# Block 2 of a fused attention and GEGLU kernel: output products at its opening, other loading order for batches 3 and 4, earlier sums of the output weights

## The chip, the cores and the metric

The kernel runs on one core of a Trainium2 chip. A core has five engines that work side by side, each through its own list of instructions in the order of the program: TensorE (PE in the profile) multiplies matrices out of SBUF into PSUM, VectorE (DVE) and ScalarE (ACT) work elementwise and read PSUM, GpSimd (POOL) works elementwise on SBUF, and SyncE (SP) here only issues DMA transfers. An instruction waits for semaphores of the work it depends on, and all that stands behind it in its engine's list waits with it. The metric is the device time of one execution in microseconds (us); lower is better. Several executions are made, and their median is the time of a kernel.

## What is computed

Eight batches go through a linear attention with eight heads, and its result through a gated feed-forward layer. Cut to what matters:

```python
# q, k, v: (8, 8, 576, 64) float32; w_gate, w_val: (512, 1536); w_out: (1536, 512)
theta = np.pi / 2.0 * pos / S
def phi(x): r = np.maximum(x, 0.0); return np.concatenate([r * cos_w, r * sin_w], axis=-1)
q_p, k_p = phi(q), phi(k)
kv  = np.einsum('bhsf,bhsd->bhfd', k_p, v)
z   = np.sum(k_p, axis=2)
num = np.einsum('bhsf,bhfd->bhsd', q_p, kv)
den = np.einsum('bhsf,bhf->bhs', q_p, z)[..., None] + 1e-06
x   = (num / den).transpose(0, 2, 1, 3).reshape(B * S, H * D)     # 4608 x 512
g   = x @ w_gate
out = (0.5 * g * (1.0 + erf(g / sqrt(2))) * (x @ w_val)) @ w_out   # 4608 x 512
```

## The kernel before

**Tiles and stages.** The 4608 rows of x are taken as nine blocks of 512 (`BLK`, `n` = 0 to 8), the 1536 hidden columns as twelve units of 128 (`JT`, `jt` = 0 to 11; "unit 3" is `jt` 3). A batch has 576 rows, so blocks and batches do not coincide: block 2 holds rows 1024 to 1535, which are the end of batch 1 and the first 384 rows of batch 2; block 3 begins in batch 2 and goes on into batch 3. The batches are therefore prepared one or two blocks ahead, between the units of an earlier block.

**A batch's way to x.** `load` (L98) brings q, k and v as float32 into the three slots of `st`, or into the spare tiles `sm` and `fs`; `stage` says which. `prep` (L177 on ScalarE, L179 on VectorE) clips at zero and multiplies with the sine or cosine of the position, one of nine groups of rows `j` at a time, into `phis`; `prep_both` (L191, L193) does it for q and k together. `cast_v` (L208) copies v into `vx`. `turn_q` (L222) transposes q with two DMAs on SyncE. `kv_unit` (L270) makes the products of k and v with 72 matmuls and copies them out on ScalarE (L279). `nm_unit` (L311 on TensorE, L322 to L324 on VectorE) makes 128 rows of the numerators, divides them by the denominators and writes an x tile; eight small matmuls into two PSUM banks from `b0` on. These steps together are called "numerators" below. `turn_x` (L378) transposes the x tile into `xT` of its block by DMA, on SyncE.

**A unit.** `gv_unit` (L430) multiplies a block's xT with 128 columns of the gate weights and of the value weights, four matmuls each of 512 columns, into two PSUM banks in turn (0 and 1, then 2 and 3). ScalarE takes the GELU of the gate part (L439, tile `gel`, two buffers), VectorE multiplies it with the value part into `hT` (L442). The next but one unit writes the same two banks. Units 0 and 1 of block 1 and units 0 to 3 of block 2 are made in two halves of 256 columns; block 2 makes the first halves of units 0 to 3, then the second halves.

**Output products.** The output of block `n - 1` is made during block `n`. For blocks 1 to 8 it uses a scheme of seven products in place of eight (`PROD`): `product` (L547) multiplies parts of hT, or sums of them (`h_sum`, L529, `SUMS` says at which step, tile in `sm`), with parts of the output weights, or differences of them (`wo_sum`, L492, four on VectorE, made once in block 1; "T1" overwrites a part of `wo_sb`). ScalarE copies some products (L565), VectorE adds them (L560). `o_step` makes one step of products: step 0 and step 6 have two products (12 matmuls), the others one (6 matmuls). In block 2 step 0 is products 2 and 1; product 2 reads hT of units 6 to 11 of block 1.

**What sets the order.** The order is written out by hand; there is no scheduler. `block1` and `block2` walk through the units; after each unit they call the small pieces that stand at that number. `LOADS` says after which (block, unit) loads of a batch are put on SyncE (with a range of `j`, or of heads), `SCALE` which groups of q and k of which batch are scaled (numbers from 12 on are units 0 on of block 2; the first tuple is sines on ScalarE, the second cosines on VectorE), `EARLY` which groups of batch 4 (`s` sines on ScalarE, `c` cosines, from unit 9 on also on ScalarE). `more` puts the sums of xT for block 3 (L630) on GpSimd after units 8 to 11 of block 2; from block 3 on the units too use a seven-product scheme (L650). All DMAs named here but a few of the first stage go through SyncE in order, so a turn of q, whose two issues take some 8 to 9 us of SyncE, holds up every load and x transpose behind it.

Around block 2 SyncE's order before is: turn of q of batch 2; the last x tile of batch 1; k of batch 3 and the first half of v; x tile 0 of batch 2; the second half of v; x tiles 1 and 2; q and k of batch 4, groups 0 to 4; turn of q of batch 3; x tiles 3 and 4; the rest of q and k and v of batch 4.

Of the kernel before, what the change touches and what calls it, by code (L numbers as in the profile page):

```python
# [16 lines left out]
def kernel(  # L17
# [13 lines left out]
    nc = tc.nc  # L31
# [6 lines left out]
    JT = J // 128  # L38
# [45 lines left out]
    def stage(name, b):  # L84
        early = {
            ("q", 1): 1, ("k", 1): sm, ("v", 1): fs, ("k", 2): 2, ("v", 2): 1,
            ("q", 3): fs, ("k", 3): 2, ("v", 3): sm,
            ("q", 5): 1, ("k", 5): 0, ("q", 7): 1, ("k", 7): 0,
        }
        at = early.get((name, b), "qkv".index(name))  # L90
        if isinstance(at, int):
            return st[:, at]
        return at[:, 0:NP * R * D].rearrange("p (m x) -> p m x", m=NP)
# [113 lines left out]
    def cast_v(b, m0, m1, copy, j0=0, j1=R):  # L207
        copy(  # L208
            vx[:, m0:m1, j0:j1, 0:D],
            staged["v", b][:, m0:m1, j0 * D:j1 * D].rearrange("p m (j d) -> p m j d", d=D),  # L210
        )
# [97 lines left out]
    def nm_unit(b, t, b0=6):  # L309
        for h in range(H):  # L310
            nc.tensor.matmul(  # L311
                bank(b0 + h // 4)[:, (h % 4) * (D + 1):(h % 4 + 1) * (D + 1)],
                lhsT=q_cols(b, t, h),
                rhs=kv_sb[b][:, h // 2, h % 2, :],
                start=True,
                stop=True,
            )
        nm = ps[:, b0:b0 + 2, 0:4 * (D + 1)].rearrange("p g (h d) -> p g h d", h=4)
        den = attn2.tile([128, 2, 4], FP32, name="den")
        rec = attn2.tile([128, 2, 4], FP32, name="rec")  # L320
        x = xsp.tile([128, 2, 4, D], BF16, name="x_sb")
        nc.vector.tensor_scalar_add(den, nm[:, :, :, D], EPS)  # L322
        nc.vector.reciprocal(rec, den)
        nc.vector.tensor_tensor(  # L324
            x,
            nm[:, :, :, 0:D],
            rec[:, :, :, None].to_broadcast([128, 2, 4, D]),
            op=ALU.mult,
        )
        xs[b, t] = x.rearrange("p g h d -> p (g h d)")  # L330
# [153 lines left out]
    def wo_sum(name):  # L484
        if not ts:
            ts["B11"], ts["B12"] = wo_sb[:, 0:JH, 0:CH], wo_sb[:, 0:JH, CH:C]
            ts["B21"], ts["B22"] = wo_sb[:, JH:JT, 0:CH], wo_sb[:, JH:JT, CH:C]
        x, y = {
            "T1": ("B12", "B11"), "T2": ("B22", "T1"), "T3": ("B22", "B12"), "T4": ("T2", "B21"),
        }[name]  # L490
        ts[name] = ts["B12"] if name == "T1" else weights.tile([128, JH, CH], BF16, name=name)
        nc.vector.tensor_tensor(ts[name], ts[x], ts[y], op=ALU.subtract)  # L492
# [403 lines left out]
    def js(a, b):  # L896
        return tuple(range(a, b))

    LOADS = {
        (1, 4): [(3, "k"), (3, "v", 0)], (1, 9): [(3, "v", 2)],  # L900
        (1, 11): [(4, "q", 0, 5), (4, "k", 0, 5)],
        (2, 2): [(4, "q", 5, R), (4, "k", 5, R), (4, "v")],
        (2, 9): [(5, "q", 0, 5), (5, "k", 0, 5)],
        (3, 1): [(5, "q", 5, R), (5, "k", 5, R), (5, "v")],
        (3, 9): [(6, "q", 0, 5), (6, "k", 0, 5)],
        (4, 0): [(6, "q", 5, R), (6, "k", 5, R), (6, "v")],
# [1 line left out]
        (5, 0): [(7, "q", 5, R), (7, "k", 5, R), (7, "v")],  # L908
    }
    SUMS = {  # L910
        2: {0: "1", 1: "2", 2: "34", 3: "56", 6: "78"},
        8: {i: str(i + 1) for i in range(8)},
    }
    for n in range(3, 8):
# [44 lines left out]
    def scale(b, name, sines_, cosines):  # L959
# [8 lines left out]
        5: (3, "q", js(0, 1), ()), 6: (3, "q", js(1, 3), js(0, 1)),  # L968
        7: (3, "q", js(3, 5), js(1, 3)), 8: (3, "q", js(5, 7), js(3, 6)),
        9: (3, "q", js(7, 9), js(6, 9)),  # L970
        10: (3, "k", js(0, 2), js(0, 2)), 11: (3, "k", js(2, 4), js(2, 4)),
        12: (3, "k", js(4, 6), js(4, 6)), 13: (3, "k", js(6, 8), js(6, 8)),
        14: (3, "k", js(8, 9), js(8, 9)),
    }

    def block1():
        b, n = 2, 1
        for jt in range(JT):
            i = jt - 9
            if i > 0:  # L980
                nm_unit(b, i, (6, 4, 6)[i])
                turn_x(b, i)
            if jt < 2:
                for i in range(2):
                    half, unit = divmod(2 * jt + i, 2)
                    x3 = lambda: turn_x_pe(1, 3, 5, dve_copy)
                    gv_unit(n, unit, half * HALF, HALF, between=x3 if jt == i == 0 else None)
                    j = JA + 2 * jt + i
                    prep("q", b, 1, (j,), eng=nc.scalar)
                    prep("q", b, 0, (j,))  # L990
            else:
                gv_unit(n, jt, between=(lambda: nm_unit(b, 0, 6)) if i == 0 else None)
            if i == 0:
                turn_x(b, 0)
            if jt % 3 == 1:
                flush()
            if jt == 2:
                prep("q", b, 0, (R - 1,))
                prep("q", b, 1, (R - 1,), eng=nc.scalar)
                turn_q(b)  # L1000
                nm_unit(1, NT - 1)
            if jt == 3:
                turn_x(1, NT - 1)
            if jt == 6:
                kv_unit(b)
            if jt in SCALE:
                scale(*SCALE[jt])
            if jt in (3, 4):
                cast_v(b, 2 * (jt - 3), 2 * (jt - 3) + 2, act_copy)
            if jt == 11:  # L1010
                cast_v(3, 0, 2, act_copy)
            start_loads(n, jt)
            if 4 <= jt < 8:
                wo_sum(("T3", "T1", "T2", "T4")[jt - 4])

    EARLY = {
        4: "s0 c0", 5: "s1 c1", 6: "s2 c2", 7: "s3 c3", 8: "s4 c4", 9: "s5 c5", 10: "s6 c6",
        11: "s7 c7", 12: "s8 c8",
    }

    def early(jt):
# [3 lines left out]

    def block2():
        b, n = 3, 2
        for jt in range(JT):
            if jt >= 4:
                gv_unit(n, jt, to=(2, 6) if jt == JT - 1 else None)  # L1030
            else:
                for i in range(2):
                    half, unit = divmod(2 * jt + i, 4)
                    gv_unit(n, unit, half * HALF, HALF)
                    if i == 0 and jt < 2:
                        nm_unit(2, 3 + jt)
                    if i == 0 and jt == 1:
                        turn_q(3)
            if 0 <= jt - 6 < NT:
                turn_x(b, jt - 6)  # L1040
            if jt == 0:
                cast_v(b, 2, 4, act_copy)
            if jt < JT - 1:
                o_step(n, jt)
            if 0 <= jt - 5 < NT:
                nm_unit(b, jt - 5)
            if jt + JT in SCALE:
                scale(*SCALE[jt + JT])
            if jt == 3:
                kv_unit(b)  # L1050
            early(jt)
            if jt == 1:
                turn_x(2, 3)
                turn_x(2, 4)
            start_loads(n, jt)
            if jt in (7, 8):
                m = 2 * (jt - 7)
                cast_v(4, m, m + 2, act_copy)
            more(n, jt)

    turn[0] = 1
# [128 lines left out]
```

## Time and profile before

| | before |
|---|---|
| three runs | 311.64, 311.2, 310.38 us; median 311.2 |
| the profiled execution | 312.38 us |
| its span (first to last instruction on the engines) | 310.6 us |
| TensorE busy | 298.2 us, 96% of the span, 3071 matmuls |
| VectorE, ScalarE, GpSimd busy | 228.1, 202.2, 153.4 us |
| granted TensorE clock, mean | 0.985 |
| x transposes between 54 and 126 us, issue to landing | 2.5 / 3.6 / 7.0 us (least, median, most) |
| turns of q there, issue to landing | 6.6 / 6.9 / 8.1 us each of two |
| loads into `st` there, issue to landing | 3.9 / 5.2 / 7.6 us |
| cast of half a batch's v (L208), ScalarE and GpSimd | 1149 and 1150 ns |

A busy TensorE is not one at full speed: matmuls are pipelined, a matmul of 512 columns starts 0.216 us after the one before it although one lasts 0.36 us by itself, and the clock that the throttle grants can fall. Block 1 runs from 55.7 to 79, block 2 from 81.5 to 116.8 us of the profiled execution, block 3 begins at 116.8. A time of a run is some 1.8 us above the span of its profile, and the profiled execution lies above the three runs shown.

### The profile page before, as it was taken

To read this page: it belongs to the slowest core of one execution; us is meant where nothing else is said; L and a number is where in the kernel's file an instruction comes from. 1 tells how busy PE (TensorE), PEld (TensorE's weight loads), DVE (VectorE), ACT (ScalarE), POOL (GpSimd) and SP (SyncE) were. 2 spreads that over 40 slices of the span, in tenths; PEclk is the share of its full clock that TensorE was granted. 3 is DMA by queue.
4 is the path that set the end of the run, shared out by engine and by line. 5 is a ranking of instruction groups with operands and counts; after the bars stand their busy time and mean duration, and the time that the engine had idled before them with its cause. 6 is when DMAs were issued, how large, how long until landed. Compare 5 with 4: busy or idle time off the path is not lost.

```text
span 310.6 us, 7905 instructions
## 1 busy us (share of the span) xinstructions
PE 298.2 (96%) x3071; PEld 226.9 (73%) x3071; DVE 228.1 (73%) x495; ACT 202.2 (65%) x394; POOL 153.4 (49%) x130
## 2 busy tenths in 40 slices
PE   8799999999799999999999999999999999999993
PEld 3574456755486557787878787878888988888882
DVE  5675996889776864789678967895678785766772
ACT  7765593997654397878587858785546456565530
POOL 6585430000000049646864686579965866297310
PEclk9799999999899999999999999999999999999998
DMA  7999999998988889995989699936732321203045
GB/s 268 250 182 236 322 302 396 267 155 209 257 191 109 272 193 223 134 342 149 192 157 329 155 198 132 341 85 111 121 78 48 83 43 36 58 12 70 0 87 118
DMA packets 73172, 53.66 MB, mean 173 GB/s; under 512 B 45392, under 2 KB 62544, under 8 KB 73136
## 3 DMA queue, kind: packets, MB, share of 16 engines
q1 hardware_dynamic: 63360, 41.17, 58.5%
q0 software_dynamic: 9696, 11.93, 16.8%
q8 instruction: 24, 0.39, 0.5%
q14 instruction: 12, 0.10, 0.1%
q10 hardware_dynamic: 80, 0.07, 0.1%
HBM read 37.75 MB, written 9.44 MB: 152 GB/s over the span
## 4 chain that ended last, share of the span: by engine, by line
PE 78%; DMA 6%; issue 5%; DVE 4%; ACT 2%; SPq 2%; POOL 1%; POOLq 0%; DVEq 0%; ACTq 0%
PE ps L650 29%; PE ps L547 19%; PE ps L430 18%; DMA st<-in_v_dram 5%; PE ps L463 3%; PE ps L311 3%; PE ps L270 2%; DMA xT<-x_sb 2%; PE ps L233 1%; SPq L98 1%; DVE hT L442 1%; ACT phis L177 1%; PE ps L401 1%; ACT gel L439 1%; PE ps L386 1%
## 5 line engine op out<-in xcount | busy, mean ns | idle before, releaser
L630 POOL TENSOR_TENSOR fs<-xT 128x512 bf16<-128x512 bf16 x12 | 13.9, 1159 | 78.3 <-ACT gel L439 68.5
L430 PE MATMUL ps<-xT,wg_sb 128*128 128x512 bf16 (+1 forms) x208 | 48.6, 357 | 2.3 <-DMA xT<-x_sb 2.3
L430 PE MATMUL ps<-xT,wv_sb 128*128 128x512 bf16 (+1 forms) x208 | 48.7, 357 | 0.0
L529 POOL TENSOR_TENSOR sm<-hT 128x768 bf16<-128x768 bf16 x24 | 39.4, 1641 | 17.0 <-PE ps L650 9.9
L442 DVE TENSOR_TENSOR hT<-gel,ps 128x512 bf16<-128x512 f32 (+1 forms) x52 | 32.3, 623 | 16.0 <-PE ps L430 10.9
L650 PE MATMUL ps<-fs,ws 128*128 128x256 bf16 x288 | 41.7, 273 | 0.0
L650 PEld LDWEIGHTS <-ws 128*128 128x128 bf16 x384 | 36.2, 98 | 4.6 <-ACT ps L669 0.3
L439 ACT ACTIVATE gel<-ps 128x512 f32<-128x512 f32 (+1 forms) x52 | 28.5, 548 | 13.7 <-PE ps L430 12.3
L682 ACT ACTIVATE gel<-ps 128x512 f32<-128x512 f32 x30 | 17.9, 597 | 30.0 <-PE ps L650 30.0
L547 PEld LDWEIGHTS <-sm 128*128 128x128 bf16 x336 | 32.9, 98 | 5.9
L650 PE MATMUL ps<-xT,wg_sb 128*128 128x256 bf16 x240 | 36.0, 273 | 0.0
L690 DVE TENSOR_TENSOR ps<-fs,ps 128x512 f32<-128x512 f32 x30 | 20.9, 696 | 20.0 <-PE ps L650 13.7
L547 PEld LDWEIGHTS <-hT 128*128 128x128 bf16 x288 | 28.7, 100 | 5.7
L430 PEld LDWEIGHTS <-wv_sb 128*128 128x128 bf16 x208 | 20.4, 99 | 16.8
L560 DVE TENSOR_TENSOR o_sb<-sm,ps 128x256 f32<-128x256 f32 x56 | 23.4, 419 | 12.0 <-ACT sm L565 10.0
L430 PEld LDWEIGHTS <-wg_sb 128*128 128x128 bf16 x208 | 19.3, 98 | 15.8 <-issue 2.8
L529 POOL TENSOR_TENSOR sm<-hT,sm 128x768 bf16<-128x768 bf16 x12 | 19.7, 1644 | 15.5 <-PE ps L547 13.1
L324 DVE TENSOR_TENSOR x_sb<-ps,rec 128x512 bf16<-128x512 f32 x38 | 26.3, 691 | 1.3
L650 PEld LDWEIGHTS <-wg_sb 128*128 128x128 bf16 x240 | 23.1, 98 | 5.4
L177 ACT ACTIVATE phis<-st,sin_t 128x256 bf16<-128x256 f32 (+1 forms) x57 | 23.9, 480 | 3.3 <-DMA st<-in_k_dram 3.3
L191 ACT ACTIVATE phis<-st,sin_t 128x512 bf16<-128x512 f32 x36 | 25.8, 717 | 0.0
L547 PE MATMUL ps<-wo_sb,hT 128*128 128x256 bf16 x192 | 24.7, 279 | 0.0
(127 smaller groups left out, 590.9 us busy)
## 6 DMA issues: line engine op xcount, KB each, us to landing
out_dram<-o_sb SPq DMA_DIRECT2D x69, 128.0 KB, 3.1
st<-in_v_dram SPq DMA_DIRECT2D x10, 576.0 KB, 7.2
st<-in_q_dram SPq DMA_DIRECT2D x5, 640.0 KB, 4.5
st<-in_q_dram SPq DMA_DIRECT2D x5, 512.0 KB, 5.0
st<-in_k_dram SPq DMA_DIRECT2D x4, 640.0 KB, 6.0
st<-in_k_dram SPq DMA_DIRECT2D x4, 576.0 KB, 4.2
st<-in_q_dram POOLq DMA_DIRECT2D x4, 576.0 KB, 12.6
st<-in_k_dram SPq DMA_DIRECT2D x4, 512.0 KB, 4.9
```

Of the source, the lines that this page charges most:

```text
L177: nc.scalar.activation(o, i, AF.Relu, scale=tab[:, j:j + 1])
L191: nc.scalar.activation(o, i, AF.Relu, scale=tab[:, j:j + 1])
L324: nc.vector.tensor_tensor(x, nm[:, :, :, 0:D], rec[:, :, :, None].to_broadcast([128, 2, 4, D]), op=ALU.mult,)
L430: nc.tensor.matmul(bank(to[g])[:, 0:w], lhsT=wt[:, ct, js], rhs=xt[:, ct, c0:c0 + w], start=(ct == 0), stop=(ct == CT - 1),)
L439: nc.scalar.activation(gel[:, 0:w], bank(to[0])[:, 0:w], AF.Gelu)
L442: nc.vector.tensor_mul(hT[n][:, jt, c0:c0 + w], gel[:, 0:w], bank(to[1])[:, 0:w])
L529: eng.tensor_tensor(a[name][:, j0:j1], a[x][:, j0:j1], a[y][:, j0:j1], op=op)
L547: nc.tensor.matmul(at, lhsT=hs.setdefault(key, h_parts(n, p))[a][:, j], rhs=ts[b][:, j], start=(j == 0 and i in ((1, 2, 4, 5), (1, 4, 5))[ ...
L560: nc.vector.tensor_tensor(o, got[key, k], x, op=op)
L650: nc.tensor.matmul(to[:, 256 * half:256 * half + 256], lhsT=w_part(a, j * 128, (j + 1) * 128)[:, ct], rhs=xb[self.n][b][:, ct], start=(hal ...
L682: nc.scalar.activation(self.gel0, self.other, AF.Gelu)
L690: nc.vector.tensor_tensor(bank(val), self.m5, self.sum, op=ALU.add)
```

## The change

Everything lies in blocks 1 and 2.

- `block2` makes output step 0 ahead of its first unit, not after unit 0; the numerators of x tile 3 of batch 2 move from block 2's unit 0 to the end of block 1, those of tile 4 from unit 1 to unit 0, and the turn of q of batch 3 with them. The banks of numerators 0, 1, 2 in block 1 change from 6, 4, 6 to 4, 6, 4.
- The four sums of the output weights move from units 4 to 7 of block 1 to units 0 to 3.
- v of batch 3 goes to `fs` (where q of batch 3 lay) instead of `sm`. Its first half is loaded after unit 9, its second after unit 11, each behind the x tiles of that unit. The last x tile of batch 1 is turned after unit 5, behind k of batch 3.
- Cosines of k of batch 3 leave block 1's units 10 and 11; sines go three, two, two, one, one and cosines three, three, three from block 2's unit 0 on. The casts of v of batch 3 move to block 2's units 1 and 2.
- The first groups of q and k of batch 4 are loaded after block 2's unit 0, behind the turn of q of batch 3, instead of after block 1's unit 11. Their scaling starts at unit 6 instead of unit 4, with one more cosine on ScalarE. v of batch 4 is cast on GpSimd after units 8 and 9, instead of on ScalarE after units 7 and 8. The first groups of batch 5 are loaded after unit 10 instead of 9.
- One sum of hT moves from step 6 to step 4 of block 2.

```diff
--- before.py
+++ after.py
@@ -84,7 +84,7 @@
     def stage(name, b):
         early = {
             ("q", 1): 1, ("k", 1): sm, ("v", 1): fs, ("k", 2): 2, ("v", 2): 1,
-            ("q", 3): fs, ("k", 3): 2, ("v", 3): sm,
+            ("q", 3): fs, ("k", 3): 2, ("v", 3): fs,
             ("q", 5): 1, ("k", 5): 0, ("q", 7): 1, ("k", 7): 0,
         }
         at = early.get((name, b), "qkv".index(name))
@@ -897,10 +897,10 @@
         return tuple(range(a, b))
 
     LOADS = {
-        (1, 4): [(3, "k"), (3, "v", 0)], (1, 9): [(3, "v", 2)],
-        (1, 11): [(4, "q", 0, 5), (4, "k", 0, 5)],
+        (1, 4): [(3, "k")], (1, 9): [(3, "v", 0)], (1, 11): [(3, "v", 2)],
+        (2, 0): [(4, "q", 0, 5), (4, "k", 0, 5)],
         (2, 2): [(4, "q", 5, R), (4, "k", 5, R), (4, "v")],
-        (2, 9): [(5, "q", 0, 5), (5, "k", 0, 5)],
+        (2, 10): [(5, "q", 0, 5), (5, "k", 0, 5)],
         (3, 1): [(5, "q", 5, R), (5, "k", 5, R), (5, "v")],
         (3, 9): [(6, "q", 0, 5), (6, "k", 0, 5)],
         (4, 0): [(6, "q", 5, R), (6, "k", 5, R), (6, "v")],
@@ -908,7 +908,7 @@
         (5, 0): [(7, "q", 5, R), (7, "k", 5, R), (7, "v")],
     }
     SUMS = {
-        2: {0: "1", 1: "2", 2: "34", 3: "56", 6: "78"},
+        2: {0: "1", 1: "2", 2: "34", 3: "56", 4: "7", 6: "8"},
         8: {i: str(i + 1) for i in range(8)},
     }
     for n in range(3, 8):
@@ -968,9 +968,9 @@
         5: (3, "q", js(0, 1), ()), 6: (3, "q", js(1, 3), js(0, 1)),
         7: (3, "q", js(3, 5), js(1, 3)), 8: (3, "q", js(5, 7), js(3, 6)),
         9: (3, "q", js(7, 9), js(6, 9)),
-        10: (3, "k", js(0, 2), js(0, 2)), 11: (3, "k", js(2, 4), js(2, 4)),
-        12: (3, "k", js(4, 6), js(4, 6)), 13: (3, "k", js(6, 8), js(6, 8)),
-        14: (3, "k", js(8, 9), js(8, 9)),
+        10: (3, "k", js(0, 3), ()), 11: (3, "k", js(3, 5), ()),
+        12: (3, "k", js(5, 7), js(0, 3)), 13: (3, "k", js(7, 8), js(3, 6)),
+        14: (3, "k", js(8, 9), js(6, 9)),
     }
 
     def block1():
@@ -978,7 +978,7 @@
         for jt in range(JT):
             i = jt - 9
             if i > 0:
-                nm_unit(b, i, (6, 4, 6)[i])
+                nm_unit(b, i, (4, 6, 4)[i])
                 turn_x(b, i)
             if jt < 2:
                 for i in range(2):
@@ -989,7 +989,7 @@
                     prep("q", b, 1, (j,), eng=nc.scalar)
                     prep("q", b, 0, (j,))
             else:
-                gv_unit(n, jt, between=(lambda: nm_unit(b, 0, 6)) if i == 0 else None)
+                gv_unit(n, jt, between=(lambda: nm_unit(b, 0, 4)) if i == 0 else None)
             if i == 0:
                 turn_x(b, 0)
             if jt % 3 == 1:
@@ -999,23 +999,23 @@
                 prep("q", b, 1, (R - 1,), eng=nc.scalar)
                 turn_q(b)
                 nm_unit(1, NT - 1)
-            if jt == 3:
+            if jt == 5:
                 turn_x(1, NT - 1)
             if jt == 6:
                 kv_unit(b)
+            if jt < 4:
+                wo_sum(("T3", "T1", "T2", "T4")[jt])
             if jt in SCALE:
                 scale(*SCALE[jt])
             if jt in (3, 4):
                 cast_v(b, 2 * (jt - 3), 2 * (jt - 3) + 2, act_copy)
             if jt == 11:
-                cast_v(3, 0, 2, act_copy)
+                nm_unit(b, 3, 6)
             start_loads(n, jt)
-            if 4 <= jt < 8:
-                wo_sum(("T3", "T1", "T2", "T4")[jt - 4])
 
     EARLY = {
-        4: "s0 c0", 5: "s1 c1", 6: "s2 c2", 7: "s3 c3", 8: "s4 c4", 9: "s5 c5", 10: "s6 c6",
-        11: "s7 c7", 12: "s8 c8",
+        6: "s0 c0 s1 c1", 7: "s2 c2 s3", 8: "c3 s4", 9: "c4 s5", 10: "c5 s6", 11: "c6 s7",
+        12: "c7 s8 c8",
     }
 
     def early(jt):
@@ -1025,6 +1025,7 @@
 
     def block2():
         b, n = 3, 2
+        o_step(n, 0)
         for jt in range(JT):
             if jt >= 4:
                 gv_unit(n, jt, to=(2, 6) if jt == JT - 1 else None)
@@ -1032,20 +1033,19 @@
                 for i in range(2):
                     half, unit = divmod(2 * jt + i, 4)
                     gv_unit(n, unit, half * HALF, HALF)
-                    if i == 0 and jt < 2:
-                        nm_unit(2, 3 + jt)
-                    if i == 0 and jt == 1:
+                    if jt == i == 0:
+                        nm_unit(2, 4)
                         turn_q(3)
             if 0 <= jt - 6 < NT:
                 turn_x(b, jt - 6)
-            if jt == 0:
-                cast_v(b, 2, 4, act_copy)
-            if jt < JT - 1:
+            if 0 < jt < JT - 1:
                 o_step(n, jt)
             if 0 <= jt - 5 < NT:
                 nm_unit(b, jt - 5)
             if jt + JT in SCALE:
                 scale(*SCALE[jt + JT])
+            if jt in (1, 2):
+                cast_v(b, 2 * jt - 2, 2 * jt, act_copy)
             if jt == 3:
                 kv_unit(b)
             early(jt)
@@ -1053,9 +1053,9 @@
                 turn_x(2, 3)
                 turn_x(2, 4)
             start_loads(n, jt)
-            if jt in (7, 8):
-                m = 2 * (jt - 7)
-                cast_v(4, m, m + 2, act_copy)
+            if jt in (8, 9):
+                m = 2 * (jt - 8)
+                cast_v(4, m, m + 2, nc.gpsimd.tensor_copy)
             more(n, jt)
 
     turn[0] = 1
```

## The prediction

> **What bounds the kernel now.** I read the page first, then TensorE's waits, the chain of waits near the longest of them, and there the timeline and one-microsecond windows.
>
> ```profile
> span 310.6 us, 7905 instructions
> PE 298.2 (96%) x3071; PEld 226.9 (73%) x3071; DVE 228.1 (73%) x495; ACT 202.2 (65%) x394; POOL 153.4 (49%) x130
> ```
>
> TensorE is the bound; only its idle or slow time can be won. Its waits (engine, line, what for: total us, times, longest):
>
> ```profile
> PE ps L430 <- DMA xT<-x_sb: 2.3, 1, 2.3
> ...
> PE ps L311 <- DVE x_sb L324: 0.8, 2, 0.5
> ```
>
> All three lie where this change works: the first at block 2's opening, the other two in block 2. The chain of waits there (start, us, what) runs through VectorE into one transposing DMA:
>
> ```profile
> 74.46 0.79 DVE phis L179 x3
> 75.25 0.09 DVE den L322
> ...
> 76.31 5.07 DMA xT<-x_sb
> 81.39 0.14 issue
> 81.52 1.03 PE ps L430 x8
> ```
>
> The timeline shows what that wait cost and who stood beside it:
>
> ```profile
> 78.17 1.03 PE L430 MATMUL ps<-xT,wv_sb 128*128 128x512 bf16 x4
> ...
> 79.44 0.91 ACT L177 ACTIVATE phis<-st,sin_t 128x256 bf16<-128x256 f32 x2 [2.46 <-DMA st<-in_k_dram]
> ...
> 80.26 0.58 ACT L439 ACTIVATE gel<-ps 128x512 f32<-128x512 f32 x1
> ...
> 81.03 0.68 DVE L442 TENSOR_TENSOR hT<-gel,ps 128x512 bf16<-128x512 f32 x1
> ```
>
> ScalarE waited 2.46 us for k of batch 3, so unit 11's GELU came at 80.26 and its hT at 81.03. In the windows (length, PE, PEld, DVE, ACT, POOL, granted clock, DMA share, GB/s) the clock falls after the idle time:
>
> ```profile
> 80.00:81.00 1.00, 0.00 (x0) 0.00 (x0) 0.93 (x4) 1.00 (x3) 0.00 (x0) 1.00 0.59 123
> 81.00:82.00 1.00, 0.48 (x5) 0.46 (x6) 1.00 (x4) 1.00 (x3) 0.00 (x0) 1.00 1.02 348
> 82.00:83.00 1.00, 1.00 (x17) 0.86 (x15) 0.25 (x2) 0.95 (x2) 0.00 (x0) 0.86 1.14 303
> 83.00:84.00 1.00, 1.00 (x6) 0.75 (x5) 0.93 (x4) 0.34 (x2) 0.00 (x0) 0.50 0.85 126
> ```
>
> Later in the timeline stand the two L311 waits, with ScalarE's wait for v of batch 4 between them:
>
> ```profile
> 106.45 0.42 PE L311 MATMUL ps<-kv_sb,qT 128*128 128x65 bf16 x8 [0.25 <-DVE x_sb L324]
> ...
> 108.96 1.16 ACT L208 CAST vx<-st 128x1152 bf16<-128x1152 f32 x1 [3.04 <-DMA st<-in_v_dram]
> ...
> 112.42 0.42 PE L311 MATMUL ps<-kv_sb,qT 128*128 128x65 bf16 x8 [0.54 <-DVE x_sb L324]
> ```
>
> What there is to win, in the profiled execution:
> - Idle at the opening: matmuls of 512 columns start 0.216 us apart, so TensorE was free at 78.17 + 0.86 = 79.03 and went on at 81.52: 2.49.
> - Slow clock: from 82.65 to 86.50 (3.85 us) it did a half unit (0.87 at full clock, 86.50 to 87.37) and 12 output products (1.31, 102.08 to 103.39): 3.85 - 2.18 = 1.67.
> - The two L311 waits: products begun at 105.38 and 111.07 take 0.66, the numerators came at 106.45 and 112.42: 0.41 + 0.69 = 1.10. The second follows ScalarE's late cast, whose wait held unit 8's GELU until 110.02.
>
> Sum 5.26. After 117 us TensorE shows no further wait, so a shift there reaches the end.
>
> **The change, part by part.** Steps between VectorE's operations are read from its timeline, start to next start, as 0.87 for a weight sum:
>
> ```profile
> 69.19 0.95 DVE L492 TENSOR_TENSOR wo_sb<-wo_sb 128x1536 bf16<-128x1536 bf16 x1
> 70.06 0.68 DVE L442 TENSOR_TENSOR hT<-gel,ps 128x512 bf16<-128x512 f32 x1
> ```
>
> So also hT 0.59 (0.33 for a half unit), three cosines 0.79 (one 0.33), one set of numerators (L322 to L324) 1.04.
>
> *Weight sums into units 0 to 3.* VectorE was busy there already. Counted on from 57.38, with a sum after each of units 0 to 3: the last cosine of q of batch 2 ends 0.4 later (62.6), hT of unit 3 ends at 65.99, of unit 4 at 68.24. The value products of units 5 and 6 need those banks; they began at 65.67 and 67.39, and now at 66.05 and 68.30: 0.91, of which 0.10 was already spent waiting for v's cast ahead of kv (68.25 to 68.35). Cost 0.8. Bounds: 0 if VectorE's steps close up, 4 x 0.87 = 3.5 if no sum is hidden.
>
> *Block 2 opens with products.* Numerators 3 of batch 2 (0.26) and 12 products (1.31) now fill the wait for x. But the products need unit 11's hT. VectorE, freed of the sums, starts hT of unit 8 when TensorE ends it (73.25 + 0.05) and then does 4 x 0.59 + 2 x 0.79 + 3 x 1.04 = 7.06; with the last one's end (0.10) and handover (0.06), 80.52, against TensorE free at 79.03 + 0.26 = 79.29. New idle 1.23, both ends moved by the 0.8. Bounds: 0.71 (hT 11 alone: 79.20 + 0.05 + 0.69 + 0.06) and 1.9 (k late, rival 2). The first half unit then starts at 79.29 + 1.23 + 0.8 + 1.31 = 82.63 with 1.57 of work behind it that stood ahead at 81.52: 83.09 - 82.63 = 0.46 won.
>
> *k ahead of v, v behind the x tiles, cosines of k out of block 1.* SyncE's turn of q (62.48, 8.33 us) starts 0.4 later, so k is issued at 71.2 and 71.7 (72.81 before). Its halves landed 4.9 and 6.0 us after issue, with v behind them; so 77.7 at the latest, when the GELU of unit 10 ends on ScalarE. x 0 of batch 2 is ready at 76.6; with its 5.07 again it lands at 81.7, 0.9 before it is needed. v's first half waits on SyncE until q's last cosine leaves fs (78); behind it is x 1, ready only at 79. x 2, ready at 80.7, is needed at 82.63 + 4 x 0.87 + 0.26 + 0.66 = 87.0; its kind landed in 2.9 to 4.8 here. v's second half, issued near 82, lands by 89 (7.1 is the longest); ScalarE casts it near 90.5, kv follows at 91.8. The rest of batch 1's last x tile goes behind k, lands in 2.9 and is needed at 82.63. Numerators 2 read the banks that the products overwrite, but x 2 comes before hT 11 on VectorE. Taken as 0, because these covers stand; each us beyond them costs a us.
>
> *The clock.* The idle 1.23 stands in for 2.49. The nearest rows: the other fall (11 to 15 us) followed 1.25 + 0.17 + 0.51 us of idle, and 0.69 at 111.7 brought none. 1.23 is nearer to 0.69 than to 1.93: no fall, 1.67 won. Bounds 0 and 1.67.
>
> The Trainium skill ("TensorE: Matmul & The Clock Gate", section "Why this matters for your kernels") asks for no idle gap over about 3 us. By that rule neither gap would touch the clock, and the sum would be 1.67 smaller; the rows above disagree with it, since 2.49 brought 0.50.
>
> *Batch 4.* Its first loads go behind q's turn on SyncE, which now starts when numerators 4 of batch 2 end (83.9; 87.86 before) and takes 9.5: issued near 94 (82.43 before), landed by 100.6 (6.0). Two x transposes (1.25 each) later come the second halves (about 98; landing 5.1) and v (7.1): 104 and 107. First use is now VectorE after x 1 of batch 3, near 102.7, ScalarE's second halves after unit 9's GELU, near 108.8. Margins 2 and 4 us. The casts (2 x 1.15 on POOL, same length as ScalarE's) stand ahead of and between the x sums; T2 was ready 2.9 before its product, so 1.15 fits. One sum (0.47) leaves VectorE's unit 6. So the two L311 waits go, up to a rest of 0.1 (bounds 0 and 1.10). Batch 5's first loads, one unit later, are first used in block 3 near 120 and issued near 113 (landing 6.1): 0. ScalarE has one more cosine before the turn of q of batch 4, 0.6 later; that landed at 132.1 and is used at 132.93: 0.
>
> The skill's "SBUF — State Buffer" ("SBUF: two separate sides") has VectorE and GpSimd share a port pair that one instruction holds alone; by it a cast could hold a cosine for up to 1.15. No run here shows such a pair, and the sum leaves it out.
>
> **Sum:** 5.26 - 0.8 - 1.23 - 0.1 = 3.1 us. The profiled execution took 312.38 (1.8 around its span), so 309.3; it stands 1.2 over the median 311.2, so the forecast for the median is 308.1.
>
> **Rivals.**
> 1. The clock falls all the same. For: 1.23 lies between the rows, on none, and the waits at 66 and 68 come before it. Against: half of the idle time that brought a fall is gone. 308.1 + 1.67 = 309.8.
> 2. The transfer is not earlier: k lands 7.6 us after issue (the longest into st in this stage) at 79.3, three sines (1.2) and the GELU (0.60) follow, hT 11 ends at 81.9, idle 1.9, and the clock falls: 308.1 + 0.7 + 1.67 = 310.5. For: ScalarE waited for just this load. Against: it is issued 1.6 earlier and v no longer shares the queue.
> 3. Slower: batch 4 comes too late behind q's turn. Place: ScalarE's sines of its second halves, with unit 10's GELU behind them and TensorE behind that. Each us past 108.8 costs a us, so it decides from 111.9; with twice the longest landing of this stage (15.2) they come at 98 + 15.2 = 113.2, and the kernel takes 308.1 + 4.4 = 312.5. For: 3.4 MB now start 11 us later, among x's transposes. Against: no load of this stage took over 7.6.
> 4. Nothing is won: VectorE hides none of the sums (3.5 in place of 0.8), 308.1 + 2.7 = 310.8.
>
> **How the numbers follow.** Forecast 0.62, rival 1 0.14, rival 2 0.10, rival 3 0.08, rival 4 0.06. The forecast's own range: 0 for the front and 0.71 for the hole win 1.3 more (306.8); 1 us on one of the covers loses as much (309.1). Rivals 1, 2 and part of 4 are taken in: 306.8 to 311.0. A measurement of this kernel tells about 0.5% (1.56 us) from no change, so faster means under 309.6: the forecast and a third of rival 1, 0.67. Slower means over 312.8: half of rival 3 and a tail of rivals 2 and 4, 0.10. The rest, 0.23, is within.
>
> **What would show it.** Right: TensorE's wait for xT gone; one idle of about 1.2 us before L547 at 80 to 81.5, released by DVE hT L442; granted clock 1.00 from 80 to 90; waits of some 0.4 us near 66 and 68; L208 on POOL near 106, no ScalarE wait for v; unit 4 of block 2 near 93 in place of 95.3. Wrong: clock 0.50 after 82; ScalarE waiting for k past 78; ScalarE or VectorE waiting for q or k of batch 4; TensorE still at the xT wait.

## The result, and the profile after

The changed kernel took 310.03 us in the median of 20 runs (308.80 to 312.85), beside 311.91 for the kernel before in 20 runs of the same chip: ratio 0.9947, 95% interval 0.9927 to 0.9968. That is a gain of 1.65 us (1.0 to 2.3). The forecast was 308.1 in a range of 306.8 to 311.0. The direction and the range held, the size was half of what was forecast. By the prediction's own measure it is no "faster" (under 309.6, given 0.67) but lies in the band around it that was given 0.23. Part of the distance from 308.1 is the starting point: the forecast went out from 311.2, the median of three runs, and 20 runs of the same kernel gave 311.91.

The profiled execution took 309.43 us. Its page:

```profile
span 307.4 us, 7903 instructions
PE 296.6 (96%) x3071; PEld 225.2 (73%) x3071; DVE 227.8 (74%) x494; ACT 200.8 (65%) x393; POOL 157.2 (51%) x132
```

The span is 3.2 us shorter than before, TensorE as full as it was. Its waits (engine, line, what for: total us, times, longest), as far as they lie where the change works:

```profile
PE ps L430 <- ACT gel L439: 0.8, 1, 0.8
...
PE ps L547 <- DVE x_sb L324: 0.5, 1, 0.5
PE ps L430 <- DVE hT L442: 0.4, 1, 0.4
```

The wait for xT and both waits of L311 are gone. Three smaller ones stand there now. The last two were forecast in kind, the first was not. TensorE's timeline shows them in place:

```profile
67.68 1.02 PE L430 MATMUL ps<-xT,wv_sb 128*128 128x512 bf16 x4 [0.37 <-DVE hT L442]
...
79.31 0.42 PE L311 MATMUL ps<-kv_sb,qT 128*128 128x65 bf16 x8
80.25 1.54 PE L547 MATMUL ps<-wo_sb,hT 128*128 128x256 bf16 x12 [0.52 <-DVE x_sb L324]
81.63 0.60 PE L430 MATMUL ps<-xT,wg_sb 128*128 128x256 bf16 x4
```

Numerators 3 are through at 79.31 + 0.26 = 79.57, the products begin at 80.25: TensorE is idle for 0.68 where it was for 2.49. Behind it the granted clock (the third figure from the end of each window) stays whole, here and in all windows up to 90:

```profile
82.00:83.00 1.00, 1.00 (x18) 0.92 (x16) 0.77 (x2) 0.59 (x2) 0.00 (x0) 1.00 1.27 182
83.00:84.00 1.00, 1.00 (x12) 0.90 (x10) 0.93 (x5) 0.60 (x2) 0.00 (x0) 1.00 0.65 111
```

The new wait lies in block 3, outside the two blocks that the change edits. The chain of waits there (start, us, what):

```profile
114.92 5.32 DMA st<-in_k_dram
120.24 0.03 ACTq L191
120.27 0.04 issue
120.31 0.72 ACT phis L191
121.04 0.49 ACT gel L439
121.53 0.04 issue
121.57 1.02 PE ps L430 x4
```

The load of k of batch 5 ends at 120.24, ScalarE's scaling waits for it, the GELU behind the scaling comes late, and TensorE's next unit with it. ScalarE's timeline has that wait:

```profile
118.45 0.61 ACT L686 ACTIVATE gel<-ps 128x512 f32<-128x512 f32 x1
120.31 0.72 ACT L191 ACTIVATE phis<-st,sin_t 128x512 bf16<-128x512 f32 x1 [1.25 <-DMA st<-in_k_dram]
```

In the changed kernel these two loads were issued at 112.83 and 114.92, behind block 3's start at 112.55. In the kernel before they were issued side by side and ahead of it (116.79):

```profile
113.70 0.52 SPq L98 DMA_DIRECT2D st<-in_q_dram  x1
114.28 0.49 SPq L98 DMA_DIRECT2D st<-in_k_dram  x1
```

**A ruler that runs do not blur.** The first 55 us differ from one execution to the next by up to 2 us, though of all kernels of this study only one (experiment 11) changes anything in them. So the traces are compared from block 1's first L430 matmul on. Times in us after that matmul, worked out from each trace's timeline:

| kernel | block 1 starts at | kv product | first half unit of block 2 | unit 4 | block 3 | end of span |
|---|---|---|---|---|---|---|
| before | 55.65 | 12.70 | 25.87 | 39.67 | 61.14 | 254.95 |
| changed | 55.22 | 13.41 | 26.41 | 36.98 | 57.33 | 252.18 |
| changed, traced again | 55.07 | 13.41 | 26.41 | 36.98 | 57.34 | 252.33 |

Three traces of the changed program (experiment 6 gave the third) agree within 0.03 us up to block 3 and within 0.5 at the end. By it the change won 61.14 - 57.33 = 3.81 us up to block 3 and lost 1.04 again behind that point: 2.77 in all. The other 0.43 of the 3.2 is block 1's earlier start, which is chance.

The span is not all of a run's time. A run lies 1.73 to 1.86 us above its span in all 63 runs of the kernel before that have both figures, and 1.99 to 2.10 in all 44 of the changed one, so some 0.26 us were lost outside the span. The prediction took 1.8 for both; what the 0.26 are is not shown.

### The profile page after: what moved, and what is told of

Its sections match the earlier page's. It is cut to its first block, busy times and chain, and to the rows that moved or that the text cites. A ratio compares the mean times of both kernels' runs of the same rounds, so it can differ in the third digit from the quotient of the medians.

```text
span 307.4 us, 7903 instructions
## 1 busy us (share of the span) xinstructions
PE 296.6 (96%) x3071; PEld 225.2 (73%) x3071; DVE 227.8 (74%) x494; ACT 200.8 (65%) x393; POOL 157.2 (51%) x132
## 4 chain that ended last, share of the span: by engine, by line
PE 83%; DMA 5%; DVE 4%; issue 4%; ACT 1%; SPq 1%; POOL 1%; POOLq 0%; ACTq 0%; DVEq 0%
PE ps L650 28%; PE ps L430 24%; PE ps L547 20%; PE ps L463 3%; PE ps L311 3%; DMA st<-in_v_dram 3%; PE ps L270 2%; DMA st<-in_k_dram 2%; PE ps L233 1%; PE ps L401 1%; SPq L98 1%; PE ps L386 1%; DVE hT L442 1%; POOL st L529 1%; DVE phis L179 1%
## 5 line engine op out<-in xcount | busy, mean ns | idle before, releaser
L430 PE MATMUL ps<-xT,wv_sb 128*128 128x512 bf16 (+1 forms) x208 | 48.2, 354 | 1.2 <-ACT gel L439 0.8
L430 PE MATMUL ps<-xT,wg_sb 128*128 128x512 bf16 (+1 forms) x208 | 48.3, 354 | 0.0
L208 POOL CAST vx<-st 128x1152 bf16<-128x1152 f32 x8 | 9.2, 1148 | 63.6 <-DMA st<-in_v_dram 63.6
L430 PEld LDWEIGHTS <-wv_sb 128*128 128x128 bf16 x208 | 20.2, 98 | 18.3 <-issue 1.9
L430 PEld LDWEIGHTS <-wg_sb 128*128 128x128 bf16 x208 | 19.3, 98 | 13.0
L324 DVE TENSOR_TENSOR x_sb<-ps,rec 128x512 bf16<-128x512 f32 x38 | 26.3, 691 | 1.3
L547 PE MATMUL ps<-wo_sb,hT 128*128 128x256 bf16 x192 | 23.8, 273 | 0.5 <-DVE x_sb L324 0.5
```

The lines of the kernel that those rows point to most:

```text
L324: nc.vector.tensor_tensor(x, nm[:, :, :, 0:D], rec[:, :, :, None].to_broadcast([128, 2, 4, D]), op=ALU.mult,)
L430: nc.tensor.matmul(bank(to[g])[:, 0:w], lhsT=wt[:, ct, js], rhs=xt[:, ct, c0:c0 + w], start=(ct == 0), stop=(ct == CT - 1),)
L547: nc.tensor.matmul(at, lhsT=hs.setdefault(key, h_parts(n, p))[a][:, j], rhs=ts[b][:, j], start=(j == 0 and i in ((1, 2, 4, 5), (1, 4, 5))[ ...
```

## The experiments

**1. The clock by itself.** The kernel before, with matmuls of no use in the idle time at block 2's opening:

```diff
+        for _ in range(8):
+            nc.tensor.matmul(bank(4), lhsT=wg_sb[:, 0, 0:128], rhs=wg_sb[:, 0, 0:BLK], start=True, stop=True)
```

> The kernel before with eight matmuls of no use (8 x 0.216 = 1.7 us) at the opening of block 2, inside the 2.49 us in which TensorE waited for x. Nothing else changes. Theory A: the clock falls there in only some executions, so keeping TensorE busy wins a part of 1.67 us, 0.3 to 1.1 us in the median (0.9965 to 0.999). Rival B: the fall comes in every execution, and the gain that is missing from the result is lost elsewhere: then 1.7 us are won (0.9945). If neither holds, no change.

Measured: 310.44 us (309.59 to 312.06, 12 runs), ratio 0.9965 (0.9941 to 0.9989), so 1.1 us won (0.3 to 1.8). Its timeline at the opening:

```profile
79.65 1.89 PE L1029 MATMUL ps<-wg_sb 128*128 128x512 bf16 x8
83.04 0.60 PE L430 MATMUL ps<-xT,wg_sb 128*128 128x256 bf16 x4 [1.50 <-DMA xT<-x_sb]
```

One of its windows behind that (the granted clock is the third figure from the end):

```profile
84.00:85.00 1.00, 1.00 (x17) 0.92 (x16) 0.49 (x2) 0.65 (x3) 0.00 (x0) 1.00 1.41 222
```

The x tile is still waited for (TensorE idle from 81.38, eight starts of 0.216 us after 79.65, to 83.04, so for 1.66 us at a stretch), and no window from there to 90 shows less than the full clock. On the ruler the first half unit starts at 26.77, which is 0.90 later than before (in this trace the tile came later), and unit 4 at 38.90, which is 0.77 earlier. Between these two marks 0.90 + 0.77 = 1.67 us were won, the price that the prediction had worked out for one fall of the clock (one trace against one; block 3 begins 0.89 earlier).

What the prediction left out is how often it falls. One fall of 3.4 us to half clock takes 0.0055 off the mean of a 310 us span. Five of 63 runs of the kernel before show a mean of 1.000, so the fall does not come in every execution. How often it comes is an estimate: the mean granted clock was 0.9919 over these 63 runs and 0.9952 over 44 of the changed kernel, which is 0.0033 or 0.6 falls; against the 0.9963 of the 12 runs with filler it is 0.8. Both figures count falls anywhere in an execution. By these figures the term is worth some 1.0 to 1.3 us on average and 1.67 only in a trace like the one that was read. The times alone do not settle it: the interval of the filler's gain, 0.3 to 1.8, takes in Rival B's 1.7.

**2. Batch 5's first loads.** The changed kernel with one number set back:

```diff
-        (2, 10): [(5, "q", 0, 5), (5, "k", 0, 5)],
+        (2, 9): [(5, "q", 0, 5), (5, "k", 0, 5)],
```

> The changed kernel with the first loads of batch 5 after unit 9 of block 2 again, not after unit 10. Theory: the 0.8 us that TensorE waits in block 3 for the GELU held behind k of batch 5 come from this step alone; they go, and the kernel is 0.8 us faster than the changed one (0.992 of the kernel before). Rival: the wait is a matter of SyncE's queue as a whole and stays; no difference from the changed kernel (0.9947).

Measured three times: 308.30 (ratio 0.9908, 0.9875 to 0.9941), 307.85 (0.9898, 0.9866 to 0.9930), 308.62 (0.9902, 0.9874 to 0.9930), six runs each. All three are under the changed kernel. SyncE's queue in the changed kernel:

```profile
111.58 1.15 SPq L453 DMA_DIRECT2D out_dram<-o_sb  x2
112.83 1.64 SPq L98 DMA_DIRECT2D st<-in_q_dram  x1
114.92 0.37 SPq L98 DMA_DIRECT2D st<-in_k_dram  x1
```

and with the loads after unit 9:

```profile
109.11 0.52 SPq L98 DMA_DIRECT2D st<-in_q_dram  x1
109.69 0.48 SPq L98 DMA_DIRECT2D st<-in_k_dram  x1
110.29 1.30 SPq L378 DMA_TRANSPOSE xT<-x_sb  x1
111.69 1.45 SPq L453 DMA_DIRECT2D out_dram<-o_sb  x2
```

The loads now stand ahead of one x transpose and of two stores, which wait for their output tile. ScalarE's timeline has the sine between the two GELUs, with no wait for its load any more:

```profile
117.49 0.61 ACT L686 ACTIVATE gel<-ps 128x512 f32<-128x512 f32 x1
117.99 0.72 ACT L191 ACTIVATE phis<-st,sin_t 128x512 bf16<-128x512 f32 x1
118.79 0.60 ACT L439 ACTIVATE gel<-ps 128x512 f32<-128x512 f32 x1
```

On the ruler the three traces end at 251.34, 251.18 and 251.35, block 3 beginning at 57.32 to 57.34 as in the changed kernel: all of the gain lies behind block 3's start.

**3. The sums of the output weights back in units 4 to 7**, the rest as changed:

```diff
-            if jt < 4:
-                wo_sum(("T3", "T1", "T2", "T4")[jt])
+            if 4 <= jt < 8:
+                wo_sum(("T3", "T1", "T2", "T4")[jt - 4])
```

> The changed kernel with the four sums of the output weights after units 4 to 7 of block 1 again. Theory: VectorE hides them no better at the front; TensorE keeps the 0.8 us there, but hT of unit 11 comes only 0.3 us earlier than in the changed kernel because VectorE is 0.5 behind at unit 8, and the idle at the opening grows to 1.7 us: 0.3 us faster than the changed kernel where the clock holds (0.9937). Rival: the longer idle makes the clock fall in more executions, and it is slower than the changed kernel by 0.3 to 1.4 us (0.996 to 0.999).

Measured: 309.41 us (308.86 to 310.00, 6 runs), ratio 0.9929 (0.9902 to 0.9956). Its waits:

```profile
PE ps L430 <- ACT gel L439: 1.6, 1, 1.6
...
PE ps L547 <- DVE x_sb L324: 0.9, 1, 0.9
```

The front stall is gone (kv product at 12.71 in place of 13.41) and 0.42 of it comes back at the opening, so block 3 starts 0.28 earlier (57.05). On the ruler that gain was eaten by the wait for k of batch 5, here 1.6 in place of 0.8. The earlier start of block 3 makes 0.28 of this; the rest is the load, which was issued 0.15 later (114.28 - 54.43 = 59.85 against 59.70) and took longer to land. This trace ends at 252.77, later than those of the changed kernel, while the median of the runs is lower; the two intervals overlap, so runs do not tell this kernel from the changed one.

**4. The opening products behind the first half units**, where step 0 stood before, the rest as changed:

```diff
-        o_step(n, 0)
...
-            if 0 < jt < JT - 1:
+            if jt < JT - 1:
```

> The changed kernel with output step 0 after unit 0 of block 2 again; all loads and everything else as changed. Theory A: the other loading order alone brings x tile 0 in time (issued 76.2, landing 3 us later, needed at 79.6), the products at the opening only add a wait for hT of unit 11, and this is 0.5 to 0.8 us faster than the changed kernel (0.992). Rival B: the products are what hides the transfer; without them TensorE waits up to 1.5 us for x, and this is 0.5 to 1.5 us slower than the changed kernel (0.9965 to 0.9995).

Measured: 310.96 us (309.35 to 311.65, 12 runs), ratio 0.9972 (0.9943 to 1.0001). Neither theory came as it was stated:

```profile
79.42 0.60 PE L430 MATMUL ps<-xT,wg_sb 128*128 128x256 bf16 x4
79.85 0.60 PE L430 MATMUL ps<-xT,wv_sb 128*128 128x256 bf16 x4
81.64 0.42 PE L311 MATMUL ps<-kv_sb,qT 128*128 128x65 bf16 x8 [1.19 <-DVE x_sb L324]
```

The half unit starts with no wait for x, so the other order of loads brought the tile in time without the products' help. But numerators 4, next in line, use the banks of numerators 3 and wait 1.19 us for VectorE to read these. What the products fill, then, is the time in which VectorE catches up. They are worth 0.69 (unit 4 at 37.67 in place of 36.98). The clock stayed whole behind this wait too.

**5. The two edits 2 and 3 together.**

> The changed kernel with two edits: batch 5's first loads behind unit 9 of block 2 (as before the change) and the sums of the output weights behind units 4 to 7 (as before the change). From the traces of the two edits made alone: sums late take the front stall away (kv product 0.70 us earlier, counted from block 1's start) and give 0.4 back at block 2's opening (products' wait 0.94 in place of 0.52), so 0.3 is won; the earlier loads win the 0.8 us wait for the GELU of line 439. Theory A (the two add up): 307.9 to 308.3 us at a before of 311.9, some 0.3 below the kernel with the early loads alone; TensorE waits of 0.9 at the products and none at the front or in block 3. Rival B (the sums only shift the wait, nothing is won): equal to the kernel with early loads alone within 0.2. Rival C (sums late make VectorE late in units 4 to 7 and the products' wait grows past 1.2): slower than early loads alone by 0.3 or more.

Measured: 308.43 us (307.40 to 310.10, 6 runs), ratio 0.9913 (0.9879 to 0.9948). On the ruler block 3 starts at 57.04 and the span ends at 250.92, the least of all traces and 0.3 under edit 2 alone, as Theory A has it. The runs do not show it (edit 2 alone had 307.85 beside these), so the 0.3 stands on the traces alone, one against three.

**6. Batch 5's first loads after unit 11.** It was meant as a dose:

```diff
-        (2, 10): [(5, "q", 0, 5), (5, "k", 0, 5)],
+        (2, 11): [(5, "q", 0, 5), (5, "k", 0, 5)],
```

> The changed kernel with batch 5's first loads behind unit 11 of block 2 in place of unit 10. These loads have a turn of q of batch 4 (9.7 us of SyncE's queue) behind them and x's transposes ahead. Theory A (the wait of ScalarE for k of batch 5 in block 3, and of TensorE behind it, comes from when that load is issued): q and k are issued 0.5 to 2 us later, TensorE's wait behind the GELU of line 439 grows from 0.8 to between 1.3 and 3, and the kernel takes 310.5 to 312.2 us at a before of 311.9. Rival B (the load's landing is held up by other traffic, not by its issue): wait stays at 0.8 within 0.3 and the time stays at 310.0. Rival C (the loads fall behind the turn of q on SyncE's queue): issued some 10 us later, a wait of 8 us or more.

Measured: 309.97 us (308.81 to 313.03, 12 runs), ratio 0.9963 (0.9930 to 0.9996). SyncE's queue gets nothing between unit 10 and unit 11, so this is the changed kernel's own list of instructions, and no dose. It serves as a repetition: q of batch 5 issued at 57.59 on the ruler (57.61 in the changed kernel), k at 59.22 (59.70), and TensorE's wait 0.5 (0.8). In the third trace of this program (experiment 9) k was issued at 59.59 and the wait was 0.9. So the wait differs by 0.4 between executions of one program, and the issue of k does not order the three by itself: the time to landing (5.5, 5.3 and 5.6) counts too.

**7. v of batch 4 cast on ScalarE again**, with edit 2 (and the two sums of hT in one step again):

```diff
-            if jt in (8, 9):
-                m = 2 * (jt - 8)
-                cast_v(4, m, m + 2, nc.gpsimd.tensor_copy)
+            if jt in (7, 8):
+                m = 2 * (jt - 7)
+                cast_v(4, m, m + 2, act_copy)
```

> The changed kernel with batch 5's first loads behind unit 9, and v of batch 4 cast on ScalarE behind units 7 and 8 of block 2, as before the change (and the two state sums together in unit 6). In the kernel with early loads alone the two halves of v land at 105.0 and 109.4, unit 7's GELU ends near 103.9 and unit 8's at 106.5, so ScalarE would wait 1.1 and 2.4 us and cast for 1.15 each time. Theory A (the step of the prediction: the late cast held the GELU of unit 8 and with it the numerators, two waits of 1.10 in all, which the move to GpSimd took away): the waits of line 311 come back, together with new ones behind the GELUs of units 8 and 9, in all 1.1 to 2.5 us; 309.3 to 310.8 us at a before of 311.9. Rival B (ScalarE's slack covers the casts; the two waits went because the numerators moved): no more than 0.3 slower than with early loads alone.

Measured: 309.76 us (308.38 to 310.68, 12 runs), ratio 0.9946 (0.9921 to 0.9971). The two waits are back:

```profile
103.60 0.42 PE L311 MATMUL ps<-kv_sb,qT 128*128 128x65 bf16 x8 [0.25 <-DVE x_sb L324]
109.60 0.42 PE L311 MATMUL ps<-kv_sb,qT 128*128 128x65 bf16 x8 [0.56 <-DVE x_sb L324]
```

They are as long as before the change (0.25 and 0.54), and block 3 starts 1.12 us later than with edit 2 alone (58.45 and 57.33). The prediction had 1.10 for this term. The edit also puts the two sums of hT back, so the figure is for both together. The runs lie 1.9 over those of edit 2 taken beside them, the trace 1.0 over edit 2's at the end of the span.

**8 and 9. Repetitions of edit 2 and of the changed kernel.**

> The kernel of the earlier run again (the changed kernel with batch 5's first loads behind unit 9 of block 2), as the measure for the others of this call. Its traced spans differed from the changed kernel's by 1.8 us, but 0.96 of it lay ahead of block 1, where neither edit reaches, so the edit itself is worth the wait of 0.8 us. Theory A: ratio to before 0.992 (0.9947 less 0.8 us), 309.2 us at a before of 311.9. Rival B (the wait hid a second loss, as the 6 runs of the first time say): 308.3 again, ratio 0.9908 or below.

> The changed kernel as it is, beside the others of this call. (The run with the loads behind unit 11 turned out to be this program too: between unit 10 and unit 11 SyncE's queue gets nothing else.) From block 1's start to the end its trace took 252.2 us and the kernel with early loads 251.3 and 251.2, but the medians of runs differ by 2.0. Theory A (the wait for k of batch 5 explains 0.9, the rest is chance between runs): 0.7 to 1.3 above the kernel with early loads in this call. Rival B (the wait is longer in executions that are not traced): 1.7 to 2.3 above it.

> The kernel with batch 5's first loads behind unit 9 once more, as the measure for the sums on GpSimd and for the changed kernel of this call. It gave 308.3 and 307.85; 308.0 +- 0.5 is expected, and 251.2 to 251.4 us from block 1's start to the end of its trace.

Measured: edit 2 as given above; the changed kernel 309.71 us (308.87 to 311.75, 12 runs), ratio 0.9942 (0.9917 to 0.9966), 1.1 above edit 2 beside it, which is Theory A of that run; the second run of edit 2 (0.9898) had come as its Rival B. Over all runs the changed kernel has a median of 309.83 (44 runs) and edit 2 308.13 (18 runs): 1.7 apart, with an interval of 0.75 to 2.1 from redrawing the runs. The three traces of each differ by 0.8 at the end of the span (252.18, 251.82, 252.33 and 251.34, 251.18, 251.35). So 0.8 is shown to come from the place of the loads, through the wait for k. Whether executions that are not traced wait longer, or the rest is chance, stays open.

**10. The loads of batch 5 behind the turn of q**, a true dose this time:

```diff
-        (2, 10): [(5, "q", 0, 5), (5, "k", 0, 5)],
-        (3, 1): [(5, "q", 5, R), (5, "k", 5, R), (5, "v")],
+        (3, 1): [(5, "q", 0, 5), (5, "k", 0, 5), (5, "q", 5, R), (5, "k", 5, R), (5, "v")],
```

> The changed kernel with batch 5's first loads behind the turn of q of batch 4 on SyncE's queue (issued in block 3's second slot, with the second loads after them), so some 12 us later: the turn took 9.7 from 116.6 in the changed kernel's trace. Theory A (what block 3 waits for is when these loads are issued; each us later costs a us): issued near 126.5, landed near 132, where their first reader stood ready at 119.06; TensorE waits 10 to 13 us behind the GELU of line 439 and the kernel takes 319 to 324 us. Rival B (the wait of 0.8 was one of several that hide each other, and other work fills a longer one): under 316.

Measured: 323.45 us (322.18 to 323.80, 6 runs), ratio 1.0370 (1.0340 to 1.0400), 13.7 above the changed kernel beside it. SyncE's queue:

```profile
116.03 8.61 SPq L222 DMA_TRANSPOSE qT<-phis  x2
124.70 0.85 SPq L98 DMA_DIRECT2D st<-in_q_dram  x1
125.62 0.48 SPq L98 DMA_DIRECT2D st<-in_k_dram  x1
```

ScalarE's timeline:

```profile
131.53 0.72 ACT L191 ACTIVATE phis<-st,sin_t 128x512 bf16<-128x512 f32 x1 [13.01 <-DMA st<-in_k_dram]
```

A window behind it:

```profile
135.00:136.00 1.00, 1.00 (x7) 0.69 (x6) 0.45 (x1) 0.46 (x1) 0.00 (x0) 0.50 1.06 394
```

On the ruler k is issued at 125.62 - 54.67 = 70.95, against 59.70 in the changed kernel: 11.25 later. TensorE's wait grew from 0.8 to 12.5, so by 11.7: about one us for each us of delay. The span ends 14.5 later on the ruler (266.83 and 252.33); the other 2.8 go with the half clock, which lasts to 138.7 in the windows.

**11. The sums of the output weights on GpSimd**, with edit 2:

```diff
-        nc.vector.tensor_tensor(ts[name], ts[x], ts[y], op=ALU.subtract)
+        nc.gpsimd.tensor_tensor(ts[name], ts[x], ts[y], op=ALU.subtract)
```

> The changed kernel with batch 5's first loads behind unit 9, and the four sums of the output weights on GpSimd in place of VectorE, still in units 0 to 3. GpSimd has nothing to do between 45 and 105 us in the trace of the kernel with early loads alone; its sums of 128x768 take 1.64 us, so 128x1536 are estimated at 3.3 each, four of them done by about 71, long before the first product (79.3). Theory A (VectorE's 3.5 us of sums are what makes units 5 and 6 wait): the waits ahead of the kv product go (0.7 won from block 1's start to the kv product, 12.7 in place of 13.4), the idle at block 2's opening stays at 0.5, and the time from block 1's start to the end falls from 251.3 to 250.6; median 0.7 below early loads alone. Rival B (GpSimd's sums slow VectorE's operations beside them): VectorE's hT multiplications or cosines of that stretch take longer than 0.68 and 0.35, and the gain is gone or turned round: within 0.3 of early loads alone, or slower.

Measured: 314.65 us (313.58 to 314.91, 6 runs), ratio 1.0092 (1.0066 to 1.0118), 6 us above edit 2 beside it. GpSimd began the sums at 48 us, as soon as the output weights had landed, because nothing in its own queue held them back to units 0 to 3. Its timeline:

```profile
55.22 3.10 POOL L492 TENSOR_TENSOR T<-wo_sb 128x1536 bf16<-128x1536 bf16 x1
58.40 3.08 POOL L492 TENSOR_TENSOR T<-T,wo_sb 128x1536 bf16<-128x1536 bf16 x1
```

VectorE's timeline of the same stretch:

```profile
55.73 0.69 DVE L324 TENSOR_TENSOR x_sb<-ps,rec 128x512 bf16<-128x512 f32 x1
56.34 2.13 DVE L179 TENSOR_SCALAR phis<-st,cos_t 128x256 bf16<-128x256 f32 x1
58.39 0.41 DVE L390 COPY xT<-ps 128x512 bf16<-128x512 bf16 x1
58.72 3.17 DVE L179 TENSOR_SCALAR phis<-st,cos_t 128x256 bf16<-128x256 f32 x2
```

A cosine takes 0.34 us elsewhere in this trace. Here the first ends at 58.47, 0.15 after GpSimd's sum, and the next two at 61.89, 0.41 after the next sum. The operations that read PSUM (L324, L390) kept their length beside the same sums. VectorE's copy of xT behind the cosines came late, TensorE waited 3.8 us for it, and the clock fell to half until 67.7. Rival B is shown for the cosines (no hT multiplication ran beside these two sums), and turned the gain round by 6 us.

## Why the prediction was right and wrong

**Right in kind.** *Front:* 0.8 was forecast, 13.41 - 12.70 = 0.71 measured. *The two L311 waits:* 1.10 forecast, 1.12 by experiment 7; GpSimd's first cast began at 105.90, forecast near 106:

```profile
105.90 1.14 POOL L208 CAST vx<-st 128x1152 bf16<-128x1152 f32 x1 [60.03 <-DMA st<-in_v_dram]
```

*Loads of batch 3:* no wait of TensorE for x, so rival 2 fell. *Batch 4:* its first loads were issued at 92.67, forecast near 94, and TensorE, VectorE and ScalarE waited for none of them, so rival 3 fell. *Clock:* whole behind the opening in all three traces of the changed program, so rival 1 fell in these. That the measured median lies by its 309.8 says nothing for it, but in executions that are not traced it stays open: the mean clock of the 44 runs, 0.9952, lies below that of the three traced ones (0.998, 0.998 and 0.997), and where these runs lost it is not known. Rival 4 fell with the front.

**The opening was better than forecast.** "But the products need unit 11's hT" was true of one product in two only, and there of the sixth matmul. VectorE's timeline:

```profile
79.51 0.69 DVE L324 TENSOR_TENSOR x_sb<-ps,rec 128x512 bf16<-128x512 f32 x1
80.12 0.68 DVE L442 TENSOR_TENSOR hT<-gel,ps 128x512 bf16<-128x512 f32 x1
```

hT of unit 11 is done at 80.80. The prediction's sum for VectorE (80.52 with its handover, 0.8 later, less the 0.43 by which block 1 started earlier: 80.89) had it right within 0.1. But TensorE began at 80.25, when numerators 2 had left their banks, and had five matmuls of 0.11 to do before it read that tile. The idle time was 1.23 - 5 x 0.11 = 0.68.

**The step that failed** is this one: "Batch 5's first loads, one unit later, are first used in block 3 near 120 and issued near 113 (landing 6.1): 0". Issued at 112.83 was right for q. But k stands behind q in the queue and was issued at 114.92, 2.1 later, and it was k that the first reader waited for. That reader was ready at 118.45 + 0.61 = 119.06, not at 120. By its own numbers the step had 120 - 113 - 6.1 = 0.9 us to spare, and took that for a cover, though rival 2 worked with a landing of 7.6. In the trace it was 119.06 - 114.92 - 5.32 = -1.18. Its price is the 0.8 of TensorE's wait, which goes when the loads go back (experiment 2). The other 0.2 of the 1.04 stays with edit 2 in two of its three traces and is no more than traces of one program differ by.

**A size that was off:** "3.85 - 2.18 = 1.67" is the price of one fall in the traces of experiment 1, but the sum took it as paid in every run. By the mean clocks, an estimate, it is 0.6 to 0.8 falls, so 0.3 to 0.7 too much.

The sum again: 3.1 forecast, + 0.55 at the opening, + 0.16 for the small rests (3.81 up to block 3), - 1.04 in block 3, - 0.3 to 0.7 for the clock, - 0.26 outside the span: 1.8 to 2.2. Measured over all runs of the study, 311.65 (83 runs) less 309.83 (44 runs) is 1.8, interval 1.3 to 2.2. In the profiled execution the errors nearly cancelled (309.3 forecast, 309.43 measured; 0.43 of it is the chance start of block 1), and so the profile by itself would have made the forecast look right. That is luck.

The version that beats both kernels is the change with batch 5's first loads left after unit 9: 308.13 us over 18 runs, and all three of its ratios lie at or under 0.991.

## What to carry to other kernels

When a change makes a stage end earlier, every load that the next stage reads is due earlier by as much; list these loads with issue, landing and first reader each by itself, the second of a pair too, and do not move them the other way. A margin smaller than the spread of landing times is no cover. A stall that is seen in one profiled execution, above all one that the clock makes, may be paid in a share of executions only, so read the mean clock of all runs before it goes into a sum.

## What the runs showed of the hardware

- VectorE's cosines from SBUF to SBUF ended 0.15 and 0.41 us after the GpSimd sums that ran beside them: one took 2.13 us and the next two 3.17 together, where one takes 0.34, while its operations on PSUM kept their usual length (0.69 and 0.41). The prediction named the Trainium skill's rule for this ("SBUF — State Buffer", section "SBUF: two separate sides": a port pair that one instruction holds alone) and said that no run showed it. The rows of experiment 11 agree with it. The change's own casts on GpSimd met no such operation: the first ran from 105.90 to 107.04, and VectorE's next cosine began at 107.17.
- 2.49 us of idle TensorE time were followed by half clock in the kernel before; 0.68 in the changed kernel and 1.66 behind 1.7 us of filler matmuls were not. In the first 55 us, where all kernels but that of experiment 11 are alike, three of 14 traces have half clock between 11 and 16 us (before, experiments 1 and 7): those whose wait at 9 us was 1.16 to 1.30. In the other eleven it was 0.80 at most. These are single executions, and no limit is shown.
- The issue of one load (q of batch 5) took SyncE 0.52 us after unit 9 and 1.64 after unit 10, with another 0.45 before the next issue, for the same bytes. Other traces with the load after unit 10 have 1.18 to 1.97; in experiment 4 it was 0.53, with 2.36 for the two stores just ahead of it in place of 1.15. The cause is not shown.
